# Own weights and scores of a linear-attention kernel in four tiles of the matrix array

## The chip, the cores and the metric

The kernel runs on one core of one Trainium2 chip. The metric is the device time of one execution in microseconds (us), the median of several runs. Before the change it is 411.36 us (three runs, 411.1 to 414.4). The profile was taken of a further execution; the span of its records is 412.3 us. A core has five engines that run side by side: TensorE (PE in the profile; its weight loads are listed apart as PEld), VectorE (DVE), ScalarE (ACT), GpSimd (POOL) and SyncE (SP), which here issues transfers between HBM and the on-chip memory SBUF. TensorE writes its results to PSUM, an accumulator memory of 128 partitions in banks.

## The reference

First comes a linear attention (RWKV-5) for 4 batches, 8 heads, 768 time steps and a head dimension of 48, then a switch layer that sends each of the 3072 tokens to one of 8 experts:

```python
for t in range(S):                                    # attention
    cur = einsum('bhd,bhe->bhde', u * k[t], v[t])
    y[t] = einsum('bhd,bhde->bhe', r[t], state + cur)
    state = w * state + einsum('bhd,bhe->bhde', k[t], v[t])
x = y.transpose(0, 2, 1, 3).reshape(B * S, H * D)     # 3072 x 384
e = argmax(x @ w_gate)                                # switch layer
out = softmax(x @ w_gate)[e] * (relu(x @ w1[e]) @ w2[e])
```

All arrays are fp32. The attention is computed in chunks of 128 steps. Within a chunk, `y` of a query step is a sum over the key steps before it, each weighted by a score (a product of a decayed `k` and a decayed `r` over the 48 dimensions), and the key of the same step has a weight of its own, the sum over d of `r * k * u`. What lies before the chunk comes in through the state.

## The kernel before

The attention runs in 32 units. A unit is one pair of heads (`hp`, 4 pairs), one half of the sequence (`hf`, three chunks, `HC = 3`) and one batch. The two heads of a pair stand one below the other in the partitions: head `hi` at partitions 64 `hi` to 64 `hi` + 47. So a matmul that contracts over one head's 48 dimensions uses only the upper or only the lower half of the array's rows (a row tile), and the two heads can be worked on at the same time.

For each unit, TensorE computes in this order (the function that emits it in brackets):

- own weights (`u_own`, matmul at line 536): for each of 3 chunks and 2 heads one matmul with a stationary operand of 48 partitions x 128 keys (`RK`, which is r times k) and a moving operand of a single column (`u`). The result is a column of PSUM tile `P0` or `P1` (one for each head, each a bank of its own).
- scores (`u_products`, line 546): for each chunk and head one matmul with a stationary `K` of 48 x 128 keys and a moving `R` of 48 x 128 queries. The result is 128 keys x 128 queries in the same `P` tile.
- state products `Gp` (`u_state`, line 582), outputs `yp` (`u_out`, lines 603 and 607), and in three units of four the gate products `rp` (`u_gate`, line 638).

Around it, GpSimd forms `RK`, `K` and `Kg` two units ahead (lines 518, 519 and 524); VectorE forms `R` (line 514), the running states `St` (line 589) and puts the scores above the diagonal into the matrix `A` (`u_mask`, line 568); ScalarE copies the own weights out of PSUM (`dv`, line 554), writes them on the diagonal of `A` (line 557), and copies `yp` and `rp` out.

The order is written out by hand (a manual schedule). In iteration `u` of the loop over units TensorE gets `u_scores(u + 1)`, `u_state(u + 1)`, `u_out(u)` and sometimes `u_gate`; VectorE gets `R` for unit `u + 2`, `St` and the mask of unit `u + 1`, and then steps of the token routing that are spread over the iterations (`todo`). There are two `P` tiles for each head, so `P` of a unit may be written while that of the unit before is still read. SyncE issues the inputs of unit `u + 5` and, between them, pieces of the expert weights.

After the 32 units, the routing of the last batch is finished, and from about 156 us on 22 tiles of 128 tokens go through the experts (`hp` at line 1072, `yp` at line 1083), with some smaller groups (`hg` at line 1132, `yg` at line 1149), which use four column tiles of 32 columns.

In the profile each fp32 matmul appears as two records of the matmul and two of the weight load.

Of the kernel before, what the change touches and what calls it, by code (L numbers as in the profile page):

```python
# [19 lines left out]
B, H, S, D = 4, 8, 768, 48  # L20
# [4 lines left out]
C = 128  # L25
# [23 lines left out]
def bc(ap, shape):  # L49
    return ap.to_broadcast(shape)  # L50
# [3 lines left out]
def rwkv5_then_switch(ctx, tc, r, k, v, rk, tok, wu_in, wg, wgh, w1, w2, out):  # L54
# [8 lines left out]
    nc = tc.nc  # L63
# [365 lines left out]
    def fast():  # L429
# [11 lines left out]
        R = Routes(ps, la, NEARLY)  # L441
# [45 lines left out]
        for u in range(NU):  # L487
            b, hf, hp = unit(u)
            x = units[u]
# [31 lines left out]
        def u_scale_g(u):  # L521
# [3 lines left out]
                x["Kg"][:, 0:ns, :], x["kt"][:, 0:ns, :],  # L525
                bc(Wg[:, hp].rearrange("p h d -> p (h d)")[:, None, :], [128, ns, 2 * D]), op=ALU.mult)

        def u_own(u):

            x = units[u]  # L530
            hp, P = x["hp"], x["P"]
            for c in range(HC):
                for hi in range(2):
                    q = slice(64 * hi, 64 * hi + D)
                    o = HC * C + c
                    nc.tensor.matmul(P[hi][:, o:o + 1], lhsT=x["RK"][q, c, :],  # L536
                                     rhs=wu[q, 1, hp:hp + 1], start=True, stop=True, skip_group_check=True)

        def u_products(u):

            x = units[u]
            P = x["P"]
            for c in range(HC):
                for hi in range(2):
                    q = slice(64 * hi, 64 * hi + D)
                    nc.tensor.matmul(P[hi][:, c * C:(c + 1) * C], lhsT=x["K"][q, c, :], rhs=x["R"][q, c, :],  # L546
                                     start=True, stop=True, skip_group_check=True)

        def u_diagonal(u):
# [9 lines left out]
        def u_scores(u, parts=(u_own, u_products, u_diagonal)):  # L559
            units[u]["P"] = [ps.tile([128, 512], FP32, name=f"P{hi}", tag=f"P{hi}", bufs=2) for hi in range(2)]  # L560
            for part in parts:
                part(u)
# [112 lines left out]
        with tc.manual_schedule():  # L675
# [6 lines left out]
            for hp in range(HP):  # L682
                scaled(W3, Wr, hp, pw[:, LV - 1])
            u_scores(0, (u_own, u_diagonal, u_products))
            tables(2)
            u_scale_first(1)
            R.begin()
            nc.vector.memset(Gp, 0.0)
            table_g()
            u_mask(0)  # L690
            u_scores(1, (u_own, u_diagonal, u_products))
            u_scale_g(0)
            load_kt(4)
# [561 lines left out]
    with tc.If(usual > 0) as which:  # L1255
        fast()
# [60 lines left out]
```

## Time and profile before

| | |
|---|---|
| time, median of 3 runs | 411.36 us |
| span of the profiled execution | 412.3 us |
| attention (32 units) | about 8.6 to 130 us |
| routing of the last batch, first tiles | 130 to 156 us |
| expert tiles | 156 to 401 us |
| records of the own weights (line 536) | 384 matmuls, mean 252 ns |
| records of the scores (line 546) | 384 matmuls, mean 290 ns |

The span is the time from the first to the last instruction. The busy time of an engine is the union of its records, so two records that overlap are counted once; the mean of a record is its whole latency, and records of the array overlap each other. What a group of matmuls costs is therefore read not from the mean of one record but from the distance between starts, or from the share of the chain of work that ended last.

### The profile page before, as it was taken

The page shows a single profiled execution, that of the slowest core. Times are in us where ns is not written, and L with a number is a line of the kernel's source. Part 1 is how long each engine was busy: PE and PEld are TensorE (multiplying, and loading weights), DVE is VectorE, ACT ScalarE, POOL GpSimd, SP SyncE. Part 2 cuts the span into 40 slices and gives each one's busy share as a digit, 9 for nine tenths or more (in the row PEclk, how much of TensorE's full clock was granted, in tenths as well). Part 3 has the DMA queues.
Part 4 walks back from the last instruction along what each step waited for, and adds up shares of the span by engine and source line. Part 5 has one row for each costly group of instructions (what it writes and reads, how often), then busy time and mean ns, then how long its engine had stood idle before and what let it go on. Part 6 is the DMA issues. An engine that isn't in the chain of part 4 may idle for free.

```text
span 412.3 us, 10590 instructions
## 1 busy us (share of the span) xinstructions
PE 398.0 (97%) x3983; PEld 328.3 (80%) x3983; DVE 241.9 (59%) x800; ACT 127.6 (31%) x395; POOL 151.2 (37%) x194
## 2 busy tenths in 40 slices
PE   7999999999999999999999999999999999999990
PEld 7899999999999777788777777777877776777770
DVE  7596788888986835444686464647444444243400
ACT  3687777777875221111101110111111011001110
POOL 6797878678770021121111212122222111110100
PEclk9699999999999999999999999999999999999995
DMA  7999989999994799569968597886868685555001
GB/s 246 272 256 272 267 219 283 282 262 308 275 288 129 242 386 367 192 207 338 335 233 298 182 289 264 255 291 207 299 219 298 234 296 192 172 187 177 33 22 29
DMA packets 42947, 99.01 MB, mean 240 GB/s; under 512 B 5189, under 2 KB 16474, under 8 KB 42882
## 3 DMA queue, kind: packets, MB, share of 16 engines
q1 hardware_dynamic: 39024, 86.94, 66.0%
q0 software_dynamic: 3712, 11.23, 9.0%
q8 instruction: 36, 0.59, 0.6%
q14 instruction: 29, 0.24, 0.2%
q10 hardware_dynamic: 146, 0.01, 0.0%
HBM read 88.72 MB, written 9.65 MB: 239 GB/s over the span
## 4 chain that ended last, share of the span: by engine, by line
PE 90%; DVE 3%; DMA 3%; SPq 1%; issue 1%; POOL 0%; ACT 0%; POOLq 0%; DVEq 0%
PE hp L1072 29%; PE yp L1083 28%; PE P L546 6%; PE P L536 6%; PE yp L607 5%; PE yp L603 4%; PE rp L638 4%; PE Gp L582 3%; DMA xs<-x_hbm,idx 2%; PE hg L1132 1%; PE yg L1149 1%; DMA w_all<-in_r_k_units_dram 1%; DVE yo L1087 0%; PE warm L484 0%; DVE Bm L986 0%
## 5 line engine op out<-in xcount | busy, mean ns | idle before, releaser
L1072 PEld LDWEIGHTS hp<-xT,w1s 128*128 128x128 f32 x1152 | 133.1, 192 | 10.4 <-issue 3.7
L1072 PE MATMUL hp<-xT,w1s 128*128 128x128 f32 x1152 | 135.2, 276 | 0.0
L1083 PE MATMUL yp<-w_all,hT 128*128 (+1 forms) x384 | 128.0, 486 | 0.0
L1083 PEld LDWEIGHTS yp<-w_all,hT 128*128 128x128 f32 x384 | 71.0, 190 | 44.2
L1074 ACT ACTIVATE hT<-hp 128x512 f32<-128x512 f32 x48 | 28.7, 597 | 219.1 <-PE hp L1072 204.5
L1007 DVE STREAM_TRANSPOSE xT<-xs 32x96 f32<-32x96 f32 x336 | 90.4, 269 | 4.9
L1094 POOL DMA_INDIRECT out_dram<-yo,idx x22 | 22.3, 1012 | 183.9 <-DVE yo L1087 175.7
L1087 DVE TENSOR_SCALAR yo<-yp,xs 128x384 f32<-128x384 f32 x22 | 13.6, 618 | 114.3 <-PE yp L1083 114.3
L557 ACT ACTIVATE A<-ident,dv 128x128 f32<-128x128 f32 x192 | 59.6, 389 | 0.2 <-ACT dv L554 0.2
L518 POOL TENSOR_TENSOR w_all<-w_all 128x384 f32<-128x384 f32 x30 | 32.5, 1082 | 22.1 <-PE P L536 5.6
L568 DVE COPY_PREDICATED A<-mask,P 128x384 f32<-128x384 int32 x64 | 36.6, 587 | 6.4 <-ACT A L557 5.7
L607 PE MATMUL yp<-A,w_all 128*64 128x128 f32 x384 | 39.0, 279 | 0.0
L1047 POOL DMA_INDIRECT xs<-x_hbm,idx x22 | 21.3, 966 | 31.1 <-DVE yo L1087 24.7
L519 POOL TENSOR_TENSOR w_all<-w_all,W 128x384 f32<-128x384 f32 x30 | 32.5, 1083 | 0.0
L603 PE MATMUL yp<-w_all,St 128*64 128x128 f32 x320 | 32.2, 278 | 0.0
L546 PE MATMUL P<-w_all 48*128 48x128 f32 x384 | 30.2, 290 | 0.5 <-ACT dv L554 0.5
L536 PEld LDWEIGHTS P<-wu,w_all 48*128 48x128 f32 x384 | 24.3, 190 | 4.3 <-issue 1.4
L536 PE MATMUL P<-wu,w_all 48*128 48x1 f32 x384 | 27.1, 252 | 0.2 <-DMA w_all<-in_r_k_units_dram 0.2
L546 PEld LDWEIGHTS P<-w_all 48*128 48x128 f32 x384 | 24.8, 192 | 0.6 <-ACT dv L554 0.6
L607 PEld LDWEIGHTS yp<-A,w_all 128*64 128x64 f32 x384 | 24.8, 140 | 0.4 <-DVE St L589 0.2
L524 POOL TENSOR_TENSOR Kg<-w_all,Wg 128x288 f32<-128x288 f32 (+1 forms) x32 | 23.9, 747 | 3.3 <-DVE Wg L478 2.8
L589 DVE SCALAR_TENSOR_TENSOR St<-St,pw,Gp 128x96 f32<-128x96 f32 x64 | 20.0, 313 | 4.1 <-PE Gp L582 2.1
(167 smaller groups left out, 289.5 us busy)
## 6 DMA issues: line engine op xcount, KB each, us to landing
w1s<-in_moe_w_dram SPq DMA_DIRECT2D x22, 1536.0 KB
wq<-in_moe_w_dram SPq DMA_DIRECT2D x32, 384.0 KB
w_all<-in_v_k_units_dram SPq DMA_DIRECT2D x64, 144.0 KB
w_all<-in_r_k_units_dram SPq DMA_DIRECT2D x56, 144.0 KB
w_all<-in_moe_w_dram SPq DMA_DIRECT2D x20, 384.0 KB
w_all<-in_moe_w_dram SPq DMA_DIRECT2D x3, 1536.0 KB
x_hbm<-xb SPq DMA_DIRECT2D x9, 385.0 KB
w1s<-in_moe_w_dram SPq DMA_DIRECT2D x8, 384.0 KB
```

The lines of the kernel that those rows point to most:

```text
L518: nc.gpsimd.tensor_tensor(x["RK"], x["r"], x["k"], op=ALU.mult)
L519: nc.gpsimd.tensor_tensor(x["K"], x["k"], bc(W2[:, x["hp"], None, :], [128, HC, C]), op=ALU.mult)
L536: nc.tensor.matmul(P[hi][:, o:o + 1], lhsT=x["RK"][q, c, :], rhs=wu[q, 1, hp:hp + 1], start=True, stop=True, skip_group_check=True)
L546: nc.tensor.matmul(P[hi][:, c * C:(c + 1) * C], lhsT=x["K"][q, c, :], rhs=x["R"][q, c, :], start=True, stop=True, skip_group_check=True)
L557: nc.scalar.activation(A[:, hi, c, :], ident, func=ACT.Copy, scale=dv[:, hi, c:c + 1])
L568: nc.vector.copy_predicated(A[:, hi], bc(mask[:, None, :].bitcast(I32), [128, HC, C]), P[hi][:, 0:HC * C].rearrange("p (c t) -> p c t", t=C))
L603: nc.tensor.matmul(yp[q, c, :], lhsT=old[:, hi, :], rhs=x["R"][:, c, :], start=True, stop=False, skip_group_check=True)
L607: nc.tensor.matmul(yp[q, c, :], lhsT=vh(x, c, hi, 64), rhs=x["A"][:, hi, c, :], start=old is None, stop=True, skip_group_check=True)
L1007: nc.vector.transpose(out[d:d + 32, :, t:t + 32], x[t:t + 32, :, d:d + 32])
L1072: nc.tensor.matmul(p[:, f, :], lhsT=self.w1[:, q, d, o:o + 128], rhs=self.xT[:, d, :], start=d == 0, stop=d == DT - 1)
L1074: nc.scalar.activation(self.hT[:, 4 * fb:4 * fb + 4, :], p, func=ACT.Relu)
L1083: nc.tensor.matmul(p, lhsT=self.hT[:, f, :], rhs=rhs, start=f == 0, stop=f == FT - 1)
```

## The change

In both functions the 128 keys of the stationary operand are split in two halves of 64. Each half gets a matmul of its own whose result goes to partitions 0 to 63 or 64 to 127 of the same PSUM tile, so that it occupies a column tile of 64 columns of the array. With the two heads as row tiles this makes four tiles of 64 rows x 64 columns, (head, half of the keys), and the four matmuls of a chunk are emitted one after the other. The aim is that the four tiles load their weights and multiply at the same time, and that each weight load, with half the columns, is shorter.

There are 12 matmuls for own weights and 12 for scores in a unit, where there were 6 and 6. The results, their places and everything that reads them are the same. On VectorE, ScalarE, GpSimd and SyncE the order of the instructions is the same in both kernels; lines below the edit move down by two.

```diff
+        quads = [(hi, j) for hi in range(2) for j in range(2)]
+
         def u_own(u):
...
             for c in range(HC):
-                for hi in range(2):
-                    q = slice(64 * hi, 64 * hi + D)
+                for hi, j in quads:
+                    q, t = slice(64 * hi, 64 * hi + D), slice(64 * j, 64 * j + 64)
                     o = HC * C + c
-                    nc.tensor.matmul(P[hi][:, o:o + 1], lhsT=x["RK"][q, c, :],
+                    nc.tensor.matmul(P[hi][t, o:o + 1], lhsT=x["RK"][q, c, t],
                                      rhs=wu[q, 1, hp:hp + 1], start=True, stop=True, skip_group_check=True)
 
         def u_products(u):
...
             for c in range(HC):
-                for hi in range(2):
-                    q = slice(64 * hi, 64 * hi + D)
-                    nc.tensor.matmul(P[hi][:, c * C:(c + 1) * C], lhsT=x["K"][q, c, :], rhs=x["R"][q, c, :],
+                for hi, j in quads:
+                    q, t = slice(64 * hi, 64 * hi + D), slice(64 * j, 64 * j + 64)
+                    nc.tensor.matmul(P[hi][t, c * C:(c + 1) * C], lhsT=x["K"][q, c, t], rhs=x["R"][q, c, :],
                                      start=True, stop=True, skip_group_check=True)
```

## The prediction

> **What bounds the kernel now.** I read the page first (busy shares, then the chain of work that ended last), then the busy times in windows, then the weight loads in order of time, then the waits. The chain, by line:
>
> ```profile
> PE hp L1072 29%; PE yp L1083 28%; PE P L546 6%; PE P L536 6%; PE yp L607 5%; PE yp L603 4%; PE rp L638 4%; PE Gp L582 3%; DMA xs<-x_hbm,idx 2%; PE hg L1132 1%; PE yg L1149 1%; DMA w_all<-in_r_k_units_dram 1%; DVE yo L1087 0%; PE warm L484 0%; DVE Bm L986 0%
> ```
>
> Nearly all of it is TensorE. The two lines that the change touches, 536 and 546, hold 6% each, some 50 of 412 us, all in the attention; the expert part (lines 1072 and 1083) is not touched. Are the other engines near their limit in the attention? The windows list for each engine its busy us in a stretch of the span:
>
> ```profile
> core 0: us, PE busy (x) PEld busy (x) DVE busy (x) ACT busy (x) POOL busy (x), PEclk, DMA share, GB/s
> 20.00:60.00 40.00, 40.00 (x746) 36.90 (x745) 30.95 (x73) 31.28 (x115) 33.97 (x38) 1.00 0.97 261
> 60.00:120.00 60.00, 60.00 (x1134) 55.74 (x1129) 52.61 (x154) 44.88 (x162) 44.09 (x48) 1.00 1.00 276
> ```
>
> TensorE never rests, but VectorE has 88% of 60 to 120 us, GpSimd 85% of 20 to 60, and the DMA share is about 1. So TensorE is the bound, with others not far behind: a gain of a tenth of the attention is about all they leave. What a group costs TensorE is seen in the weight loads (start, length, count):
>
> ```profile
> 67.98 0.79 PEld L638 LDWEIGHTS rp<-IW,y 128*64 128x64 f32 x16
> 68.90 0.75 PEld L536 LDWEIGHTS P<-wu,w_all 48*128 48x128 f32 x12
> 69.56 0.75 PEld L546 LDWEIGHTS P<-w_all 48*128 48x128 f32 x12
> 70.44 0.35 PEld L582 LDWEIGHTS Gp<-w_all,Kg 128*48 128x48 f32 x12
> 71.31 0.25 PEld L607 LDWEIGHTS yp<-A,w_all 128*64 128x64 f32 x4
> 71.53 0.25 PEld L603 LDWEIGHTS yp<-w_all,St 128*64 128x64 f32 x4
> 212.17 0.13 PEld L1132 LDWEIGHTS hg<-wq,xTg 128*32 128x32 f32 x4
> ```
>
> A single load lasts 190 ns for 128 columns, 137 for 64, 126 for 48, 109 for 32 (groups by form). Twelve loads of line 536 take 0.75 us, so (0.75 - 0.19) / 5 = 112 ns lie between one pair of loads and the next: six turns, in each of which both row tiles work. Line 546 has the same 112 ns, though its matmuls stream 128 columns instead of one; so both are set by loading 128 columns. From 68.90 to 70.44 own weights and scores cost 1.54 us a unit. The other groups show what column tiles do. `Gp` (two tiles of 48 columns): (0.35 - 0.126) / 5 = 45 ns a turn. `yp` (two tiles of 64, 128 columns streamed): two turns in 71.53 - 71.31 = 0.22, 110 ns each. `rp` (two tiles of 64, 104 streamed): 16 records are 0.71 us in the chain, 8 turns of 89 ns. And the four loads of `hg`, 109 ns each, take 0.13 together: four tiles start some 7 ns apart.
>
> A record alone streams N columns in N / 1.2 ns (line 1083: 16 records of 384 columns in 5.16 us, 322 ns each). So a turn is the longer of the streaming, N / 1.2 + 3, and the load, columns / 1.2 + 5 (128: 112; 48: 45), however many tiles share it.
>
> [...] no row shows rows and columns tiled together. [...] the page's second slice has a granted clock of 0.6[...].
>
> **The change, part by part.**
>
> Own weights: 12 matmuls, 24 records, 6 turns of four tiles. The load has 64 columns: 64 / 1.2 + 5 = 58 ns. 6 x 58 = 0.35 us, against 6 x 112 = 0.67. The trace has no such group; the lower bound is this, the upper is an issue limit. The densest run of records in the trace is `Gp`, 22.5 ns a record (45 / 2)[...]. At 22.5 the 24 records take 0.54. I take 0.35, since the four `hg` tiles start 7 ns apart[...].
>
> Scores: again 6 turns of four tiles, the first load 58 ns, then streaming 128 / 1.2 + 3 = 109 ns: 0.06 + 6 x 109 = 0.72; to that the 0.09 that lie between the last score and `Gp` now (1.54 - 12 x 0.112 - 0.107), [...], which stays (64x64 to 128x64 instead of 64x128 to 128x64). The last tile of four starts 20 ns after the first: 0.01. Sum 0.82 against 0.87.
>
> Together 1.17 us against 1.54: 0.37 a unit, 32 units, 11.8 us. It lies wholly on the path, as TensorE is full.
>
> What it moves: `P` is ready 0.37 us sooner in each period, and ScalarE's `dv`, which waits for it, starts sooner; the chain `dv`, diagonal, mask, `yp` keeps its length from there. Two waits of 20 to 130 us bear on it (total us, times, longest):
>
> ```profile
> ACT dv L554 <- PE P L546: 22.0, 24, 1.3
> DVE A L568 <- ACT A L557: 5.7, 25, 0.3
> ```
>
> ScalarE waits 0.92 us a unit for scores and so can follow. The number of PSUM buffers, waits and transfers stays; twice as many TensorE instructions cost nothing elsewhere.
>
> What does not arrive. (a) Units 2 to 5: the period is 3.05 us, GpSimd's work a unit there 2.7 to 2.95 (lines 518, 519, 524 in order of time); it can follow by 0.1 to 0.2 instead of 0.37: lost 0.8. (b) In units 12 and 13 the mask ends only 0.0 and 0.45 us before its `yp` starts (records of lines 568 and 607), as VectorE is late with routing steps: lost 0.6. (c) In 60 to 120 us the period shrinks by 16 x 0.37 = 5.9, and VectorE's 52.6 of 54.1 would be 97%; in-order waits on such an engine cost something. The mask ends 0.6 to 1.6 us before its `yp` in nearly all units, so most of it is bridged; I take 1.4 lost over all units. (d) In units 0 and 1 the clock is partly halved, each turn double: the gain there may be 0.3 more, part of it held by ScalarE's chain; taken as nothing.
>
> 11.8 - 0.8 - 0.6 - 1.4 = 9.0. The 26 us of routing and the expert tiles follow unchanged. 411.4 - 9.0 = 402.4.
>
> **Rivals.**
>
> 1. An issue limit: own weights at 22.5 ns a record, 0.54 instead of 0.35; scores are not touched (24 x 22.5 = 0.54 is under 0.66). Gain 0.18 a unit, 5.8 us, of which little is lost: 406. For it: no run of loads is denser in the trace. Against: the 7 ns.
> 2. The two column tiles of one row tile load one after the other: 2 x 53 + 5 = 112 a turn, as now. Own weights and scores cost what they do now: 411. Or another bound (VectorE, or the DMA share near 1, at 276 GB/s and needing some 305) takes nearly all: 409 to 411. Against the first: `rp` has turns of 89 ns with two loads of 53 (107 in a row). Against the second: windows of 10 us with 302 GB/s, and the slack of the masks.
> 3. Slower: the four tiles go only two at a time. Own weights 12 x 58 = 0.70, scores 12 x 109 = 1.31, so 0.67 more a unit, 21 us: 432. Against: `hg` runs four at once. [...]
>
> **How the numbers follow.** The forecast 0.62 (399 to 405), rival 1 0.16 (405 to 408), rival 2 0.12 (408 to 413), rival 3 0.10 (above 415). The time is the forecast's, 402.4. The lower end is the whole 11.8 plus the 0.3 twice: 399. The upper end takes in rival 1 with losses: 408.5. Outside are most of rivals 2 and 3, about 0.2. The 1% bound is 407.2: faster 0.78, within 0.12, slower 0.10.
>
> **What would show it.** Right: the loads of line 538 (as it is then) in groups of four within 0.02 us, 24 of them in about 0.35 + 0.1 us; 24 loads of line 548 with turns of 109; 1.17 us from the first own load to the first `Gp` load; attention ending near 121; VectorE above 90% in its middle. Wrong: turns of 90 ns or more in line 538 (rival 1), turns of 112 in both (rival 2), 24 score records over 1.2 us (rival 3). If the unit saves 0.37 and the span less than 6, a wait for masks, `RK` or inputs has taken TensorE's place.

## The result, and the profile after

The changed kernel takes 423.7 us (median; 421.6 to 425.0 in 4 runs) against 411.4 (411.1 to 414.4) of the kernel before on the same chip: a ratio of 1.028, with a 95% interval of 1.022 to 1.033. It is slower by 12.3 us where a gain of 9.0 was forecast. The first view to compare is the chain of work that ended last, by engine before:

```profile
PE 90%; DVE 3%; DMA 3%; SPq 1%; issue 1%; POOL 0%; ACT 0%; POOLq 0%; DVEq 0%
```

and by engine and by line after:

```profile
PE 80%; DVE 8%; issue 4%; DMA 4%; ACT 2%; POOL 1%; POOLq 0%; SPq 0%; DVEq 0%
PE hp L1074 28%; PE yp L1085 27%; PE yp L609 5%; PE P L548 4%; PE yp L605 4%; PE rp L640 3%; PE P L538 3%; PE Gp L584 2%; DMA w_all<-in_r_k_units_dram 2%; DMA xs<-x_hbm,idx 2%; PE hg L1134 1%; PE yg L1151 1%; DVE w_all L514 1%; ACT A L559 1%; DVE A L570 1%
```

The two changed groups fell from 6% each to 3% (line 538) and 4% (line 548), as they should. But VectorE, "issue" and the transfers (the inputs `in_r_k_units` among them) have grown in the chain, from 3%, 1% and 3% to 8%, 4% and 4%. In the windows (the same two stretches and columns as before) TensorE has fallen from full to 83% and 90%, and its granted clock to 0.96 and 0.91. No other engine has taken its place: all have less work in these stretches than before.

```profile
core 0: us, PE busy (x) PEld busy (x) DVE busy (x) ACT busy (x) POOL busy (x), PEclk, DMA share, GB/s
20.00:60.00 40.00, 33.12 (x859) 29.21 (x859) 26.52 (x62) 26.77 (x95) 29.81 (x34) 0.96 1.04 260
60.00:120.00 60.00, 54.02 (x1330) 47.49 (x1330) 50.30 (x128) 39.76 (x141) 40.65 (x43) 0.91 0.95 256
```

Is the array itself at fault? The weight loads of one unit in order of time (start, length, count):

```profile
70.92 0.44 PEld L538 LDWEIGHTS P<-wu,w_all 48*64 48x64 f32 x24
71.26 0.65 PEld L548 LDWEIGHTS P<-w_all 48*64 48x64 f32 x24
72.08 0.35 PEld L584 LDWEIGHTS Gp<-w_all,Kg 128*48 128x48 f32 x12 [0.17 <-POOL Kg L524]
```

It is not. From the first own load to the first `Gp` load there are 72.08 - 70.92 = 1.16 us, where 1.54 were; 1.17 had been worked out. The 24 records of own weights take 0.34 us to the first score load. Units that nothing disturbs have a period (first own load to the first own load of the next unit) of 3.52 us instead of 3.89, or 2.90 instead of 3.27: 0.37 less, in both.

So the time is lost between these units. The waits of 20 to 140 us (us in total, times, longest us) name it:

```profile
PEld P L548 <- issue: 7.5, 5, 3.9
PE P L548 <- issue: 5.2, 3, 3.7
PEld P L538 <- issue: 4.5, 8, 2.0
PE P L538 <- issue: 4.1, 4, 1.9
PE yp L609 <- issue: 2.1, 1, 2.1
POOL w_all L518 <- DMA w_all<-in_r_k_units_dram: 4.5, 3, 2.0
```

"Issue" is idle time for which the profile finds no releaser. The kernel before had 0.9 us of it in all on these lines, at most 0.2 at once. A timeline of TensorE's matmuls in one such place shows that the stop is no wait of the program:

```profile
85.72 0.64 PE L548 MATMUL P<-w_all 48*64 48x128 f32 x15
90.02 0.80 PE L548 MATMUL P<-w_all 48*64 48x128 f32 x9 [3.65 <-issue]
```

Fifteen of the 24 records of one group have run, nine have not, and no semaphore stands between them. A chunk has eight of these records, so the stop falls inside the second chunk, between records that read and write the same tiles: TensorE, it seems, had no next instruction. The eight longest stops add up to 12.2 us. The page has one more queue that points to the cause (packets, MB, share of 16 engines):

```profile
q8 instruction: 42, 0.69, 0.7%
```

Before it had 36 packets. The change adds 768 matmul and 768 load records; 1,536 / 6 = 256 records for each added packet, and 0.69 MB / 42 are 16 KB for each. The kernels of the experiments below fit: 768 records more than before (e1, e2, h1) come with 39 packets, 2,304 more (e3) with 45, none more (e4) with 36, while `q14 instruction` has 29 in every one of them. So this queue is taken here as the one that brings TensorE's instructions, in blocks of 256 records, one packet each. Each stop ends about 1.5 us after a packet of this queue has landed (packets and TensorE's records from the trace, us):

| TensorE stops | packet starts | has landed | TensorE goes on | after landing |
|---|---|---|---|---|
| 21.06 | 20.37 | 21.59 | 23.01 | 1.42 |
| 38.25 | 35.94 | 37.20 | 38.76 | 1.56 |
| 43.07 | 42.44 | 43.81 | 45.21 | 1.40 |
| 50.45 | 48.85 | 50.05 | 51.54 | 1.49 |
| 56.05 | 54.43 | 55.73 | 57.23 | 1.51 |
| 81.27 | 79.26 | 80.62 | 82.08 | 1.46 |
| 86.36 | 87.28 | 88.49 | 90.02 | 1.53 |
| 118.58 | 116.73 | 118.02 | 119.44 | 1.42 |

Where the stops fall settles it. TensorE's records in the trace (matmuls, weight loads and those of its sequencer) can be counted in the order of their starts: before the ends of the eight stops, 705, 1473, 1729, 1985, 2242, 3522, 3777 and 5057 of them have begun, and each of these numbers leaves 193 or 194 when it is divided by 256. In all 16 profiles of this study, units 2 to 31 have 35 stops of the matmuls of more than 0.5 us for which the profile finds no releaser. All 35 leave 193 to 195, so they lie whole blocks of 256 records apart, at block borders. The two longest waits for VectorE in e4 (below) lie elsewhere: they end after 1747 and 2870 records, which leave 211 and 54.

The packets themselves have not become slower. In the DMA view of 20 to 120 us of the kernel before the queue has

```profile
q8 instruction: 15, 0.25, 1.1%
```

and in that of the kernel after

```profile
q8 instruction: 18, 0.29, 1.4%
```

1.1% of 16 x 100 us over 15 packets are 1.2 us for each, 1.4% over 18 also 1.2. What has changed is how long a packet lasts. With 256 records for each added packet, it feeds at most 128 matmul records (each with its load). A unit had about 68 of them in a mean undisturbed period of 3.68 us, 18.5 a us, so a packet lasted 6.9 us. Now it is 92 in 3.3 us, 27.9 a us, and a packet would last 4.6.

That is short. The start of a packet follows the moment at which TensorE goes into the block before it: between 20 and 125 us by -0.4 to 5.2 us, in the median 2.3 (in the kernel before -0.2 to 3.4, median 1.3). With 1.2 us for the packet and 1.4 from its landing to its use, the median sum is 4.9 us where a block lasts 4.6; before it was 3.9 where a block lasted 6.9.

The chain in order of time (start, us, what) shows the longest stop and some of what comes after it:

```profile
86.36 3.65 issue
...
94.21 1.38 PE P L548 x24
...
102.41 4.00 DMA w_all<-in_r_k_units_dram
...
110.38 3.31 DMA w_all<-in_r_k_units_dram
```

At 94.21 the scores take 1.38 us, twice the 0.71 of other units: during the stop of 3.65 us the granted clock was halved, to 0.50 from 88.5 to 98.7 us, and after the one at 21.06 from 23.6 to 27.1. In the attention of the kernel before it was halved only from 11.4 to 18.2 us, at the start, where a turn of own weights takes up to 0.22 us instead of 0.11. The prediction reckoned with it there alone. Here it was halved after a stop of 1.94 us, and not after one of 2.14; in f2 (below), with ten stops of 0.6 to 2.1 us, the clock is 1.00 in both windows from 20 to 115 us. So the length of a single stop does not decide it, and what does was not shown. Half speed for 3.4 + 10.2 us costs at most half of that, by this estimate 6.8 us.

The account, by the distance from the first own load of unit 2 to that of unit 31: 105.7 us before, 105.7 - 29 x 0.37 = 95.0 if every period had its 0.37, and 120.9 measured. Of the 25.9 us between, 12.2 are stops and up to 6.8 the clock; the rest, 7 us or more, 4.4 of them in units 24 to 30, lies in periods that show waits for VectorE and for inputs; it was not divided among them. On the other side units 0 and 1 were 3.3 us shorter than before, since in this execution the halved clock did not fall on them.

### The profile page after: what moved, and what is told of

The parts are those of the page before. It is cut to its first block, busy times and chain, and to the rows that moved or that the text cites. A ratio compares the mean times of both kernels' runs of the same rounds, so it can differ in the third digit from the quotient of the medians.

```text
span 423.2 us, 12126 instructions
## 1 busy us (share of the span) xinstructions
PE 393.5 (93%) x4751; PEld 319.0 (75%) x4751; DVE 249.7 (59%) x800; ACT 128.5 (30%) x395; POOL 152.2 (36%) x194
## 4 chain that ended last, share of the span: by engine, by line
PE 80%; DVE 8%; issue 4%; DMA 4%; ACT 2%; POOL 1%; POOLq 0%; SPq 0%; DVEq 0%
PE hp L1074 28%; PE yp L1085 27%; PE yp L609 5%; PE P L548 4%; PE yp L605 4%; PE rp L640 3%; PE P L538 3%; PE Gp L584 2%; DMA w_all<-in_r_k_units_dram 2%; DMA xs<-x_hbm,idx 2%; PE hg L1134 1%; PE yg L1151 1%; DVE w_all L514 1%; ACT A L559 1%; DVE A L570 1%
## 5 line engine op out<-in xcount | busy, mean ns | idle before, releaser
L609 PE MATMUL yp<-A,w_all 128*64 128x128 f32 x384 | 42.7, 289 | 2.2 <-issue 2.1
L548 PE MATMUL P<-w_all 48*64 48x128 f32 x768 | 30.5, 284 | 6.6 <-issue 5.2
L605 PE MATMUL yp<-w_all,St 128*64 128x128 f32 x320 | 35.5, 288 | 0.3 <-issue 0.3
L1049 POOL DMA_INDIRECT xs<-x_hbm,idx x22 | 21.2, 966 | 33.5 <-DVE yo L1089 27.1
L609 PEld LDWEIGHTS yp<-A,w_all 128*64 128x64 f32 x384 | 28.4, 146 | 3.3 <-issue 2.2
L548 PEld LDWEIGHTS P<-w_all 48*64 48x64 f32 x768 | 22.5, 138 | 8.5 <-issue 7.5
L514 DVE TENSOR_TENSOR w_all<-w_all,W 128x384 f32<-128x384 f32 x30 | 26.4, 879 | 0.0
L524 POOL TENSOR_TENSOR Kg<-w_all,Wg 128x288 f32<-128x288 f32 (+1 forms) x32 | 25.7, 803 | 1.6 <-DVE Wg L478 1.6
L605 PEld LDWEIGHTS yp<-w_all,St 128*64 128x64 f32 x320 | 23.0, 145 | 0.8 <-issue 0.8
```

The source lines that it names most:

```text
L514: nc.vector.tensor_tensor(x["R"], x["r"], bc(W1[:, x["hp"], None, :], [128, HC, C]), op=ALU.mult)
L548: nc.tensor.matmul(P[hi][t, c * C:(c + 1) * C], lhsT=x["K"][q, c, t], rhs=x["R"][q, c, :], start=True, stop=True, skip_group_check=True)
L605: nc.tensor.matmul(yp[q, c, :], lhsT=old[:, hi, :], rhs=x["R"][:, c, :], start=True, stop=False, skip_group_check=True)
L609: nc.tensor.matmul(yp[q, c, :], lhsT=vh(x, c, hi, 64), rhs=x["A"][:, hi, c, :], start=old is None, stop=True, skip_group_check=True)
```

## The experiments

Two theories stand against each other. F: TensorE outruns the fetch of its instructions; the time goes where many records are issued in a short time, whatever they compute. O: a faster array runs into the other engines and the transfers, and "issue" is only how such waits appear. All distances below are those of units 2 to 31. Later runs look at what is left when F is out of the way.

**Own weights alone in four tiles (e1).** The scores stay as before.

```diff
-                for hi, j in quads:                                  # scores
-                    q, t = slice(64 * hi, 64 * hi + D), slice(64 * j, 64 * j + 64)
-                    nc.tensor.matmul(P[hi][t, c * C:(c + 1) * C], lhsT=x["K"][q, c, t], ...
+                for hi in range(2):
+                    q = slice(64 * hi, 64 * hi + D)
+                    nc.tensor.matmul(P[hi][:, c * C:(c + 1) * C], lhsT=x["K"][q, c, :], ...
```

> Only the own weights are cut into four tiles; the scores stay in two row tiles. Per unit 12 TensorE records more instead of 24, and 0.31 us less array time (six turns of 58 instead of 112 ns). Theory F (TensorE's instructions arrive too late, since the stream is denser): fewer and shorter stalls than in the changed kernel, so 405 to 416 us, clearly under 423.7; gaps that end some 1.5 us after an instruction packet of 16 KB has landed. Theory O (VectorE, GpSimd or the inputs cannot follow a faster TensorE): array time falls almost as in the changed kernel, so it is as slow as that, 420 to 424.

Measured 413.1 us against 413.6 of before on this chip, ratio 1.000 (0.997 to 1.003). About 80 records a unit, 23.4 a us: one stop, of 0.44 us. The undisturbed period falls from 3.89 to 3.68, which would be 6.7 us in 32 units, and yet nothing arrives: the distance is 106.3. So something other than F eats a gain here. The window of 60 to 120 us gives TensorE 94% and shows no stop of the clock:

```profile
60.00:120.00 60.00, 56.68 (x1259) 50.49 (x1257) 53.81 (x144) 43.07 (x156) 46.40 (x49) 1.00 1.00 275
```

**Scores alone in four tiles (e2).** The mirror image: line 538 as before, line 548 in quads.

> Only the scores are cut into four tiles; the own weights stay. Again 12 records more, but only 0.06 us less array time per unit. Theory F: the stream per us is denser by some 14%, between before and after, so stalls appear though TensorE is hardly faster: 412 to 418 us. Theory O: nothing changes, 409 to 411, since the pace is that of before.

Measured 414.6 against 413.6, ratio 1.003 (1.000 to 1.006), distance 109.8. Also 80 records, 21.6 a us, and no stop of more than 0.3 us at a block border: the time lies in the expected band, the expected stops did not come. In one unit it is 1.58 us from the first own load to `Gp`, no less than the 1.54 of before, so this half alone has no gain to lose. The two halves are not additive: alone they save 0.21 and nothing, together 0.37. A change of only one of them puts one more change of tiling between the two groups, and in this kernel the first score load comes 0.77 us after the first own load where it was 0.66; that the one causes the other is not shown.

**Own weights issued twice (e3).** Scores as before; the quads of the own weights are emitted two times, with the same result. The records rise to 104 a unit, while the array's own work stays near that of before.

```diff
-                for hi, j in quads:
+                for hi, j in quads + quads:
```

> The own weights are computed in four tiles and each matmul is issued twice (the second writes the same values again); the scores stay as before. Array time per unit is about that of before (12 turns of 58 = 0.70 us against 6 of 112 = 0.67), but there are 36 records more, so the density of the stream is that of the changed kernel (112 records in 3.9 us against 100 in 3.5). Theory F: slower than before by 8 us or more (420 to 435), with the same gaps behind instruction packets. Theory O: the pace of TensorE is that of before, so 411 to 413.

Measured 432.0 against 413.6, ratio 1.045 (1.033 to 1.056). The loads show that the array needs only 0.80 us for the 48 records:

```profile
76.23 0.79 PEld L538 LDWEIGHTS P<-wu,w_all 48*64 48x64 f32 x48 [0.17 <-issue]
77.03 0.75 PEld L548 LDWEIGHTS P<-w_all 48*128 48x128 f32 x12
```

The undisturbed period is 4.03 us, 0.14 longer than before: 29 x 0.14 = 4 us. The distance grew by 123.6 - 105.7 = 17.9. The waits of 20 to 135 us have the stops again:

```profile
PE P L538 <- issue: 3.0, 4, 1.3
PE P L548 <- issue: 2.1, 2, 1.4
PE yp L609 <- issue: 1.5, 1, 1.5
```

and the clock is halved twice for 3.4 us. Seven stops of more than 0.4 us stand at block borders, 6.8 us in all (for one of them, of 0.57, the profile names VectorE). With these, 4 us of array work and up to 3.4 of the clock, nearly 4 of the 17.9 remain that I can't assign. This array is slower than before, so by O nothing should run into anything. F stands; O as the cause of the stops is out.

**Both heads in one matmul (e4).** The same array time without added records: a matmul for each half of the keys contracts over both heads at once, with a moving operand of two columns (`ub`, head 0's `u` above zeros, zeros above head 1's). Scores as before.

```diff
-                for hi, j in quads:
-                    nc.tensor.matmul(P[hi][t, o:o + 1], lhsT=x["RK"][q, c, t], rhs=wu[q, 1, hp:hp + 1], ...
+                for j in range(2):
+                    t = slice(64 * j, 64 * j + 64)
+                    o = HC * C + 2 * c
+                    nc.tensor.matmul(P[0][t, o:o + 2], lhsT=x["RK"][:, c, t], rhs=ub[:, hp, :], ...
```

> The own weights of both heads in one matmul: contraction over all 128 partitions (the rows between the heads are zero), a moving operand of two columns (u of the one head and of the other, zero elsewhere), two column tiles of 64 keys. 12 records per unit as before, six turns of 58 ns instead of 112, so 0.31 us less array time without a single instruction more; ScalarE copies the six columns in one instruction instead of two. Scores as before. Theory F: no stalls or few, a gain of 6 to 10 us: 401 to 406. Theory O: a faster TensorE finds the others unable to follow, 409 to 424.

Measured 412.3 against 413.6, ratio 0.997 (0.995 to 1.000): some 11 us better than the changed kernel, and no gain on before, where F alone had 401 to 406. One stop for instructions is left, of 0.7 us (49.13 to 49.81, after 1473 records; 68 records a unit), and the undisturbed periods are those of the changed kernel (3.52, 2.88). So the added records are what makes the change a loss. But the distance is 105.2 instead of 95, and this looks like O: the window and the waits (20 to 130 us) show VectorE at 57.3 of 60 us, and GpSimd waiting 9.4 us for `r` and `k` from memory, ahead of `RK`.

```profile
60.00:120.00 60.00, 56.73 (x1088) 51.81 (x1086) 57.29 (x147) 42.39 (x139) 45.33 (x50) 1.00 1.01 281
```

```profile
POOL w_all L524 <- DMA w_all<-in_r_k_units_dram: 9.4, 9, 2.0
ACT ex L207 <- DVE sub L205: 6.6, 3, 2.7
PE P L552 <- DVE w_all L520: 2.8, 6, 0.9
```

**The changed kernel with fewer transfers in the attention (f1).** The expert weights are issued after the 32 units, not between them. The total (427.5) says nothing, since the experts now wait for their weights; the distance does.

```diff
-                for load in piece.get(u, ()):
-                    load()
...
+            for load in pieces[AHEAD:]:
+                load()
```

> The changed kernel with the transfers of the expert weights, all but the first three, issued after the 32 units instead of between them; the time to the end grows since the experts then wait, so what is compared is the distance from the first own load of unit 2 to that of unit 31 (before 105.7 us, changed kernel 120.9; 95 would be the whole gain of 0.37 a unit). Theory F, in the form that a packet of instructions queues behind the data in the DMA engines: with a third less data it lands sooner, the gaps of more than 0.3 us without a semaphore go, and the distance falls to 97 to 108. If the lateness has nothing to do with the load of the DMA engines: 115 to 121.

Distance 104.9 instead of 120.9 (115.2 in a second execution, h2 below), with the same 92 records a unit. Two of the eight stops are left (20.28 to 22.11 and 78.82 to 79.74), with the DMA share down to 0.71 and 0.74:

```profile
20.00:60.00 40.00, 38.02 (x1000) 34.16 (x1000) 31.53 (x76) 30.61 (x111) 35.02 (x40) 0.96 0.71 185
60.00:115.00 55.00, 52.67 (x1412) 46.79 (x1409) 52.15 (x138) 41.76 (x152) 45.99 (x48) 1.00 0.74 200
```

So the stops depend on the other transfers too. The packets of the instruction queue last 1.2 us here as well. What is shorter is the time from TensorE's step into a block to the start of the next packet: 1.3 us in the median, where the changed kernel has 2.3 and its second execution 2.2. Traffic is not all that sets it, since the kernel before has 1.3 at a DMA share of 1.

**The changed kernel with less VectorE work (f2).** The scaling of `R` on VectorE is left out from unit 3 on. The attention's results are then others, and with them the routing and the total (591.5 us); here and in f3, f4 and g3 only the distance is compared.

```diff
-                    if u:
-                        u_scale_r(u + 2)
```

> The changed kernel without VectorE's scaling of R from unit 3 on (the three R buffers keep the values of units 0 to 2), which takes 0.7 to 0.9 us per unit from VectorE; that part of the computation is left out. Compared: the distance from unit 2 to unit 31 (changed kernel 120.9 us). Theory F: the stalls behind instruction packets stay or grow, 108 to 118. If VectorE alone were what holds the changed kernel back: 95 to 99.

Distance 114.1, against 120.9 and 115.2 in two executions of the changed kernel: no gain clear of that scatter. Ten stops of 0.6 to 2.1 us at block borders are still there, 11.5 us in all (for two of them the profile names ScalarE or GpSimd): VectorE's load does not cause them.

**The same for the joint kernel (f3).** e4 with `R`'s scaling left out: is VectorE what held e4?

> The kernel with the joint own weights (no instruction more than before, 0.31 us less array time a unit) and without VectorE's scaling of R from unit 3 on. Its distance from unit 2 to 31 was 105.2 us with R, where 105.7 - 29 x 0.31 = 96.7 was to be had. Theory V (VectorE holds the gain back): 96 to 99. Theory D (late inputs r and k hold it back): 102 to 105.

Distance 102.6 (e4: 105.2). VectorE has fallen to 80%, and GpSimd still waits for inputs (20 to 130 us):

```profile
60.00:115.00 55.00, 52.34 (x1053) 48.82 (x1050) 44.01 (x120) 38.82 (x128) 38.83 (x44) 1.00 1.03 279
```

```profile
POOL w_all L524 <- DMA w_all<-in_r_k_units_dram: 5.4, 4, 2.4
```

By this single run, relieving VectorE alone brings 2.6 of the 10 us.

**The changed kernel with both taken away (f4).** f1 and f2 together.

> Both at once in the changed kernel: expert weights after the units, and no scaling of R from unit 3 on (left out). If instruction packets queueing behind data and VectorE are the two causes, the distance from unit 2 to 31 comes near the 95 us of the array arithmetic: 95 to 98. If a third cause is at work, it stays above 100.

Distance 100.4, above the 95 to 98 of two causes alone, and without a stop of more than 0.3 us. About half of the 5.4 us above 95.0 (2.6) sits in the periods of units 13, 21, 27 and 29, which carry routing steps: they last 4.3 to 4.65 us, where 0.37 less than before would be 3.8 to 3.9. ScalarE waits for VectorE inside the routing (in the waits, `ex` for `sub`, 5.2 us in 3 times), but it does so before the change too (4.2 us in 4 times); that this wait is the cause is not shown.

**e3 with fewer transfers (g1).** If the traffic is all that makes the fetch late, 104 records a unit should also go through.

> The kernel that issues the own weights twice (pace of the array as before, stream of instructions as dense as in the changed kernel), with the expert weights after the 32 units as in the run before. Its distance from unit 2 to unit 31 was 123.6 us, against 105.7 before the change; the array arithmetic asks for about 107. Theory F in its queueing form: with a third less data the instruction packets land in time, 106 to 111, no gap over 0.3 us without a semaphore beyond one or two. If twice the matmuls cost something by themselves: 118 or more, with the weights late too.

Distance 118.4, not the 106 to 111 that was expected; e3 had 123.6. Stops of 2.32, 0.52 and 0.79 us remain, at 169 and 196 GB/s in the two windows. The expectation had set the array's time too low: with e3's periods, 0.14 us longer than before, the distance without losses is 109.8, so 8.6 us are lost. That is no more than in f1 (9.9 above 95.0), and the run doesn't show that the rate of records does more harm at lighter traffic.

**The joint kernel with fewer transfers (g2), and with less VectorE work as well (g3).** f3's question from the other side.

> Joint own weights (no instruction more, 0.31 us less array time a unit), with the expert weights after the units; u of the two heads is now laid out by ScalarE at the start instead of by GpSimd. Compared is the distance from unit 2 to 31, 105.2 us with the weights between the units, 102.6 without VectorE's scaling of R, 96.7 by the array arithmetic. Theory D (late inputs hold the gain back): 98 to 101. Theory V (VectorE does): 103 to 105.

> The same, and without VectorE's scaling of R from unit 3 on (left out). If late inputs and VectorE together hold the gain of the joint own weights back: 97 to 99. What stays above is a third thing, the chains of the routing steps through VectorE and ScalarE: 99 to 101, with the slow periods in the units where a batch is routed.

Distances 104.8 and 99.2. With the inputs early and VectorE as it was, the units run ahead by 5.8 us up to unit 27 and give it back there: the units 27 and 29, with the last routing steps, take 6.6 and 7.4 us. With VectorE relieved alone it was 102.6; with both 99.2. The two do not add up, as each hides a part of the other. Of the 4.2 us that are left above 95.0, 3.1 sit in the periods of units 27 and 29, with the last routing steps.

**The joint kernel, with `ub` laid out before the attention by ScalarE (g4).** In e4 GpSimd laid it out at the start of the attention.

```diff
+    ub = consts.tile([128, HP, 2], FP32, name="ub")
+    nc.gpsimd.memset(ub, 0.0)
...
+    for hi in range(2):
+        q = slice(64 * hi, 64 * hi + 64)
+        nc.scalar.copy(ub[q, :, hi], wu[q, 1, :])
```

> Joint own weights as a whole kernel, with u laid out by ScalarE at the start, so that the first unit does not begin 1.2 us later than before, as it did in the first kernel with joint own weights. Array time falls by 0.31 us a unit, the number of TensorE instructions is that of before. The first one stood at 0.9975 of before. Expected 0.990 to 0.996, some 2 to 4 us faster than before; if the late start cost nothing, 0.997 to 1.000.

Measured 412.5 against 413.0, ratio 0.998 (0.996 to 1.001). The expected gain did not come, as in e4: no kernel of this study beats the one before by more than its measurement's interval.

**Joint own weights and scores in four tiles (h1).** The array time of the changed kernel or a little less, with 80 records a unit instead of 92.

> Joint own weights in two column tiles (12 records a unit) and the scores in four tiles (24 records): the array time of the changed kernel, 0.37 us a unit less than before, with 12 TensorE records a unit fewer than it has, some 24 a us instead of 28. Theory F: hardly any stall behind instruction packets, so the result is that of the other kernels without stalls, 0.995 to 1.003 of before, 409 to 415 us, and the distance from unit 2 to 31 is 103 to 108. If the faster pace of the array, not the number of instructions, makes the changed kernel slow: 1.02 to 1.03, distance 115 to 121.

Measured 413.6 against 412.6, ratio 1.001 (0.999 to 1.004), distance 108.7, just above the expected 103 to 108. With 12 records fewer in each unit the 12 us are gone. Two stops of more than 0.4 us are left, 1.92 and 0.84; for the longer the timeline of TensorE shows that it falls in the middle of a `Gp` group. A packet of the instruction queue landed at 50.17, 1.74 us before the end.

```profile
49.69 0.29 PE L589 MATMUL Gp<-w_all,Kg 128*48 128x48 f32 x4
51.91 0.25 PE L589 MATMUL Gp<-w_all,Kg 128*48 128x48 f32 x3 [1.92 <-issue]
```

**The changed kernel once more (h2).** Are the stops the same in a second execution?

> The changed kernel once more, unaltered. Theory F: again several gaps over 0.3 us without a semaphore, each ending 1.2 to 1.7 us after an instruction packet of 16 KB has landed, not at the same units as in the first profile, since they depend on the moment; distance from unit 2 to 31 of 115 to 122 us.

One run, 419.3 us, distance 115.2. Stops at 21.53 (1.70), 68.38 (0.71), 73.94 (0.65), 83.76 (1.18) and 102.03 (1.56), each ending 1.4 to 1.7 us after a packet has landed; halved clock from 24.6 to 31.5 and from 86.1 to 92.9. All five stand at block borders, two of them (after 705 and 3777 records) at the same ones as in the first profile. Of the 20.2 us above 95.0, 5.8 are stops and up to 6.8 the clock; 7.6 or more remain, much as in the first profile.

Taken together, in the order of records per us (records a unit over the mean undisturbed period):

| kernel | records a unit | per us | stops at block borders, over 0.4 us | distance, us |
|---|---|---|---|---|
| before | 68 | 18.5 | none | 105.7 |
| e4, g4 (joint) | 68 | 20.7 | one in e4, 0.7 us; none in g4 | 105.2, 105.6 |
| e2 (scores) | 80 | 21.6 | none | 109.8 |
| e1 (own) | 80 | 23.4 | one, 0.4 us | 106.3 |
| h1 (joint, scores) | 80 | 24.2 | two, 2.8 us | 108.7 |
| e3 (own twice) | 104 | 27 | seven, 6.8 us | 123.6 |
| after | 92 | 27.9 | eight, 12.2 us | 120.9 |

## Why the prediction was wrong

- **The array, right.** Turns of 58 ns for own weights and 109 for scores, four tiles at once, 1.17 us a unit: measured 1.16. In the unit at 70.92 us the loads of a turn start 7 ns apart, the turns 55 to 59 ns apart in line 538 and, from the second on, 109 to 111 in line 548. The undisturbed periods save the 0.37 that the sum rests on. Rivals 1, 2 (first part) and 3 are refuted by the same rows: slower came true, but not by tiles going two at a time.
- **The step that failed: "twice as many TensorE instructions cost nothing elsewhere".** Each 256 records more come with one more packet of `q8 instruction`, and TensorE stood at the borders of such blocks. The stops cost 12.2 us and the halved clock beside them up to 6.8; e4, which has the same undisturbed periods without the added records, has one stop of 0.7 us and is 11 us faster. The page of before held what was needed to ask: the row of queue 8 with 36 packets, and that 24 records more in a unit on 68, in a period shorter by a tenth, make a packet last 4.6 us instead of 6.9. What it could not tell is the 1.4 us from a packet's landing to its use: nothing waited for it.
- **The losses (a) to (c), 2.8 us, under-sized.** e4 shows them with hardly a stop: the distance should be 95.0 and was 105.2, so 10 us of losses and not 2.8 (g4 and h1, whose arrays are as fast, stand at 105.6 and 108.7). VectorE at 57.3 of 60 us was foreseen (97%, from 52.6 of 54.1); its price of 1.4 us was not. The slack of the masks was taken to bridge it. It does in single units (in e4, units 6 to 10 all have their saving), but units 11, 13, 20, 21, 25 to 27 and 29, with routing steps and late inputs, take it back. In its second part rival 2 named this, another bound that takes nearly all, at 0.12.
- **(a), GpSimd in units 2 to 5, not settled.** Before, the periods of units 2 to 5 sum to 12.96 us. In e4 they sum to 11.81, so 1.15 of 4 x 0.37 = 1.48 arrived and 0.33 are lost instead of 0.8; but in g4, with the same array time, they sum to 12.77, and 1.3 are lost.
- **(d), the clock at the start, taken as nothing.** Units 0 and 1 were 3.3 us shorter in the profile of after, since the halved stretch did not fall on them. It is a gain, but not one that the change can claim: the halved stretch is there in 7 of the 16 profiles, before's and e1's among them, and not in those of e2 and e3, whose arrays are no faster than before. The profiled execution of before took 414.1 us, not its median of 411.4.
- **The sentence on what would show it wrong** looked for a wait for masks, `RK` or inputs. Such waits are there (`RK`'s inputs, 4.5 us), but the larger part has no releaser at all. The forecast's conditions had no place for a wait that the program doesn't contain.

Open: what the 1.4 us from a packet's landing to TensorE's next record consist of, and what holds a packet back by up to 5.2 us after TensorE has gone into the block before. f1 shows that traffic matters, e4 and h1 that the rate of records does, not in which ratio. VectorE and late inputs can be told apart only in part, since each hides the other.

## What to carry to other kernels

Splitting a matmul over more tiles of the array bought array time with instructions here, 0.37 us a unit for 24 matmul records more: before it, divide the matmul records by the time they will take, and compare with the densest long stretch that the kernel runs without idle "issue" (here up to 22 a us there was at most one stop, of 0.7 us, at 23 and 24 one or two, at 28 eight, all at a DMA share of 0.9 or more). If TensorE is idle in the middle of a group and no semaphore ends it, look whether a packet of its instruction queue has just landed, and count its records: here all such stops lie a multiple of 256 records apart. And do not count on the room that an engine at 88% leaves next to a bound of 100%: four versions with a faster array, and no or few stops (e1, e4, g4, h1), all came out at the old time. How much of that VectorE took, and how much late inputs and the routing steps, is told apart only in part.

## What the hardware did that was not expected

- TensorE stood still where a block of its instructions ends. At 28 matmul records a us (each with its weight load), beside a DMA share of 1.04 and 0.95 in the two windows, the changed kernel has eight stops of 0.5 to 3.65 us, each ending 1.4 to 1.6 us after a 16 KB packet of `q8 instruction` that took about 1.2 us has landed; in h1 and h2 it is 1.4 to 1.74. From 20 to 125 us, in all 16 profiles, no packet starts more than 0.5 us before TensorE goes into the block ahead of it. All 35 stops over 0.5 us lie at block borders of 256 records.
- Some stops came with a halved clock: the one of 3.65 us with 10.2 us at 0.50, the one of 1.94 was followed by 3.4; that of 2.14 us at 43.07 by none, and those of f2, up to 2.1 us, left the clock at 1.00.
- Tiles in both directions worked at once in fp32: in the own weights at 70.92 us, 24 weight loads of 64 columns start within 0.31 us and their matmuls within 0.33, 14 ns each, while the densest run of 12 loads before (`Gp`) had 22.5.
- A group in four tiles next to one in two row tiles cost some 0.1 us more than next to its like: from the first own load to the first score load it is 0.77 us in e2 where it was 0.66 before, and 0.46 in e1 where the changed kernel has 0.34. The scores alone save nothing, the own weights alone 0.21 us, both 0.37.
